# Joining even and odd halves before the last Fourier stage, moving adds from GpSimd to VectorE, and reordering loads and stores, in a kernel of gated attention and spectral mixing

## The chip, the cores and the metric

The kernel runs on one core of a Trainium2 chip. The metric is the device time of one execution in microseconds (us), lower is better. The core has five engines that run side by side, each through its own stream of instructions in order: TensorE (PE, matmuls), VectorE (DVE), ScalarE (ACT), GpSimd (POOL) and SyncE (SP, which here only issues DMAs). A program on one core is called slow in single executions that lie over 1.5% above the fastest of the same kernel; those are left out of every ratio.

## The reference

`x` has 2048 rows (S) and 640 columns (D). Two branches are mixed by a gate for each row:

```python
g = sigmoid((x * gate_w).sum(-1))          # one gate per row
out = g * A(x) + (1 - g) * B(x)

def A(x):   # 32 heads of 20, four segments of 512 rows, a running linear memory
    q, k, v = heads(x @ wq), heads(x @ wk), heads(x @ wv)
    phi = lambda t: where(t > 0, t + 1, exp(t))
    for s in range(4):
        p = softmax(qs @ ks.T * scale + causal_mask)
        o = sb * (phi(qs) @ M) / (phi(qs) @ z + 1e-6) + (1 - sb) * (p @ vs)   # sb = sigmoid(beta)
        M += phi(ks).T @ vs;  z += phi(ks).sum()
    return o @ wo

def B(x):   # mixing by a two-dimensional Fourier transform
    return irfft2(rfft2(x) * (w_r + 1j * w_i))
```

The Fourier transforms are done as matmuls with cosine and sine tables. Along the rows, 2048 = 128 x 16, in two stages each way; along d, with 321 frequencies.

## The kernel before

The kernel is written by a small list scheduler in Python. Over a thousand operations are recorded with what they read and write, with the engines they may run on, and with a priority. A table `PLAN` has 1,353 numbers, each of which shifts the priority of one operation.

Work by engine: PE does all matmuls; ACT the softmax exponentials (80 of 128x2048, 150 us) and some copies out of PSUM (the memory that matmuls write, in banks); POOL the causal masks (128, 81 us) and the adds shown below; DVE the rest.

The even and odd parts over d: the result of the inverse transform over d at columns d and 640-d is E+O and E-O. The kernel before keeps both, E at `G[..., 0:322]` and O at `G[..., 322:644]`, and lets the last Fourier stage (`Fb`) join them by accumulation, with a second table that carries the opposite sign for the second half:

```python
# inverse over d: n2 = 0..15, typ 0 is E, typ 1 is O; each is copied from PSUM by ACT or DVE
self.Sc.op(copy_alts(G.ap(n2 * 644 + typ * 322, [1, KD]), psum.ap(0, [1, KD])), name="ev_Db")

# last Fourier stage of an output tile (segment s, four token phases 4a..4a+3), for each half hf of the 640 columns
for typ in range(2):
    for q in range(4):      # 32x320 matmuls, one column group of PE each
        matmul(psum[32*q:32*q+32], fb.ap((L if hf and typ else 0) + 32 * (4*a + q), [1, 32]),
               G.ap((4*a + q) * 644 + typ * 322 + 320 * hf, [1 - 2*hf, 320]), start = typ == 0)
# ... then o @ wo is accumulated into the same bank, and the bank is copied to ot
dma(dap(out, (s*L + 4*a) * D, [D, 4], [16*D, 32], [1, D]), ot.ap(0, [1, D]), name="st_out")
```

phi(t) is max(t, 0) + min(exp(t), 1), in two DVE passes and one POOL add; the spectral product is two DVE products for each bank and POOL adds; the memory part of o is added on POOL:

```python
fmin: dve  et  = min(et, 1)
fmax: dve  dst = max(q, 0)
fadd: pool dst = dst + et
for r in range(2):
    W_mul: dve  Pt[2*r + ri] = psum * Wt[r]          # 128x321
W_add: pool Yt[r] = Pt[a0] -/+ Pt[a1]                # 128x321
addmem: pool on = on + mem                           # 128x320 (the last of 24 may run on DVE)
```

At the start, one transposed load brings the first segment of x; the weights follow, then eight loads of plain x for the Fourier branch (its first step are sums and differences of rows of x, "folds", on DVE and POOL). At the end, SP waits for every DMA semaphore.

The softmax here doesn't subtract the row's maximum and nothing guards it: scores larger than these inputs give would overflow.

## Time and profile before

| | before |
|---|---|
| time, median of fast runs | 273.74 us (272.74 to 275.2, 4 runs) |
| profiled span | 270.9 us |
| PE busy / DVE / ACT / POOL | 244.7 / 204.1 / 203.3 / 192.4 us |
| mean granted PE clock | 0.985 |
| end of the last copy to end of the span | 7.9 us (270.9 - 262.96) |

First lines of the profile's page: busy time by engine with its share of the span, and the span in 40 slices of 6.8 us, where each digit is tenths of busy (9 is 90% or more; for PEclk tenths of the full clock; for DMA the mean share of 16 DMA engines).

```profile
PE 244.7 (90%) x3354; PEld 145.4 (54%) x3376; DVE 204.1 (75%) x522; ACT 203.3 (75%) x207; POOL 192.4 (71%) x256
PE   8998698679999999998989999999999999999970
DVE  0179999979999989998999999889986653444300
POOL 7058887779697675899997968798999645535200
PEclk9999979999999999999999999999999999999996
DMA  7975975264985655875544456121651443374211
```

PE is the busiest engine, and its row shows where it is not busy: in the first fifth and in the last two slices.

The same by stretches of time: the two times of the stretch, its length, busy time of each engine with the number of instructions, granted clock, DMA share, GB/s.

```profile
core 0: us, PE busy (x) PEld busy (x) DVE busy (x) ACT busy (x) POOL busy (x), PEclk, DMA share, GB/s
0.00:20.00 20.00, 17.83 (x134) 6.62 (x137) 6.43 (x12) 8.52 (x10) 9.32 (x14) 1.00 0.87 243
20.00:40.00 20.00, 16.49 (x145) 8.86 (x146) 19.27 (x37) 11.13 (x17) 16.28 (x17) 0.91 0.81 201
40.00:60.00 20.00, 14.83 (x181) 8.24 (x179) 19.51 (x45) 14.56 (x19) 14.38 (x18) 1.00 0.46 127
60.00:200.00 140.00, 133.57 (x1755) 81.56 (x1773) 131.10 (x357) 121.70 (x117) 119.88 (x167) 1.00 0.56 138
200.00:262.50 62.50, 61.94 (x1148) 40.07 (x1145) 27.75 (x74) 46.96 (x47) 32.53 (x44) 1.00 0.39 88
```

From 20 to 60 us PE idles 8.7 of 40 us while DVE is busy 38.8. From 200 us on PE is busy nearly without a gap, so work taken from PE there should shorten the run. From 60 to 200 us PE is busy 95%, DVE 94%, and POOL 86%.

Groups of instructions (line, engine, operation, tiles, shapes, count, then busy us and mean ns, then idle time before them and its releaser), the POOL adds and one DVE pass:

```profile
L1030 POOL TENSOR_TENSOR phq<-phq,et_93 128x512 bf16<-128x512 bf16 x9 | 10.6, 1172 | 2.5 <-DVE et_93 L1028 2.5
L1307 POOL TENSOR_TENSOR Yt_68<-Pt_66 128x321 bf16<-128x321 bf16 x16 | 11.7, 739 | 3.2 <-DVE Pt_66 L1302 2.2 <-DVE rs_126 L1179 0.8
L1192 POOL TENSOR_TENSOR on_106<-on_106,mem 128x320 bf16<-128x320 bf16 x15 | 11.8, 795 | 0.8 <-DVE on_106 L1184 0.8
L1028 DVE TENSOR_SCALAR et_92<-et_92 128x512 bf16<-128x512 bf16 x15 | 8.5, 567 | 0.0
```

The timeline (start, length, engine, line, operation, tiles, count, then in brackets the idle time before it and its releaser): the first load of plain x, and the last two lines of the program.

```profile
9.78 0.53 SPq L596 DMA_DIRECT2D xsb<-in_A_x_dram  x1
...
262.52 0.44 ACT L575 ACTIVATE ot_77<-psum 128x320 bf16<-128x320 f32 x1 [0.24 <-PE psum L567]
262.99 0.54 SPq L596 DMA_DIRECT2D out_dram<-ot_77  x1
```

After the last issue, 7.4 us pass until the end. In the stretch from 262.5 to 266 us the DMA share is 0.26, at 84 GB/s.

### The profile page before, as it was taken

The page shows a single profiled execution, that of the slowest core. Times are in us where ns is not written, and L with a number is a line of the kernel's source. Part 1 is how long each engine was busy: PE and PEld are TensorE (multiplying, and loading weights), DVE is VectorE, ACT ScalarE, POOL GpSimd, SP SyncE. Part 2 cuts the span into 40 slices and gives each one's busy share as a digit, 9 for nine tenths or more (in the row PEclk, how much of TensorE's full clock was granted, in tenths as well). Part 3 has the DMA queues.
Part 4 walks back from the last instruction along what each step waited for, and adds up shares of the span by engine and source line. Part 5 has one row for each costly group of instructions (what it writes and reads, how often), then busy time and mean ns, then how long its engine had stood idle before and what let it go on. Part 6 is the DMA issues. An engine that isn't in the chain of part 4 may idle for free.

```text
span 270.9 us, 8271 instructions
## 1 busy us (share of the span) xinstructions
PE 244.7 (90%) x3354; PEld 145.4 (54%) x3376; DVE 204.1 (75%) x522; ACT 203.3 (75%) x207; POOL 192.4 (71%) x256
## 2 busy tenths in 40 slices
PE   8998698679999999998989999999999999999970
PEld 2333274445646565655546566646556646655770
DVE  0179999979999989998999999889986653444300
ACT  1467345988879889899789888979887888789440
POOL 7058887779697675899997968798999645535200
PEclk9999979999999999999999999999999999999996
DMA  7975975264985655875544456121651443374211
GB/s 193 311 231 168 232 178 160 68 161 91 232 189 131 147 141 164 200 133 150 135 115 126 121 165 201 52 70 43 175 147 58 129 71 78 84 118 96 63 50 60
DMA packets 55735, 36.83 MB, mean 136 GB/s; under 512 B 31521, under 2 KB 51985, under 8 KB 55697
## 3 DMA queue, kind: packets, MB, share of 16 engines
q1 hardware_dynamic: 54384, 35.81, 53.0%
q10 hardware_dynamic: 1312, 0.49, 0.7%
q8 instruction: 26, 0.43, 0.7%
q14 instruction: 13, 0.10, 0.1%
HBM read 19.90 MB, written 9.84 MB: 110 GB/s over the span
## 4 chain that ended last, share of the span: by engine, by line
PE 59%; DVE 24%; ACT 5%; POOL 4%; DMA 4%; issue 2%; DVEq 0%; SPq 0%
PE psum L567 59%; DVE xsb L877 4%; ACT ex L1149 3%; DMA gbc<-g_scr 2%; DVE phq L1029 2%; DVE qu_90 L577 2%; DVE et_93 L1028 1%; DVE et_92 L1028 1%; DMA k_scr<-qu_90 1%; DVE phk_95 L1029 1%; DVE xf_110 L872 1%; POOL fbg_72 L980 1%; DVE va_102 L1055 1%; POOL fbg_73 L980 1%; DVE Pt_67 L1302 1%
## 5 line engine op out<-in xcount | busy, mean ns | idle before, releaser
L1149 ACT ACTIVATE ex<-psum 128x2048 bf16<-128x2048 f32 x80 | 150.1, 1877 | 23.1 <-PE psum L567 22.4
L1152 POOL TENSOR_SCALAR_AFFINE_SELECT ex<-ex 128x512 bf16<-128x512 bf16 x128 | 81.0, 650 | 41.4 <-ACT ex L1149 37.8
L567 PEld LDWEIGHTS psum<-va_102,ex 128*128 128x128 bf16 x640 | 18.1, 96 | 4.1 <-POOL ex L1152 1.2
L567 PEld LDWEIGHTS psum<-va_103,ex 128*128 128x128 bf16 x640 | 18.3, 96 | 3.5 <-issue 0.8
L567 PE MATMUL psum<-va_103,ex 128*128 128x21 bf16 x640 | 19.1, 172 | 0.7 <-DVE Cp L577 0.5
L567 PE MATMUL psum<-va_102,ex 128*128 128x21 bf16 x640 | 19.2, 173 | 0.6 <-POOL ex L1152 0.5
L567 PE MATMUL psum<-big,Ac 128*128 128x161 bf16 (+2 forms) x96 | 17.8, 318 | 0.7 <-DVE Pt_67 L1302 0.5
L567 PE MATMUL psum<-qp_98,kp_100 20*128 20x512 bf16 (+3 forms) x256 | 15.8, 301 | 1.9 <-ACT ex L1149 1.2
L567 PE MATMUL psum<-wv,xT_88 128*128 128x500 bf16 (+1 forms) x80 | 14.8, 328 | 2.8 <-DVE va_102 L1055 2.7
L567 PE MATMUL psum<-big,Cp 128*128 128x321 bf16 (+1 forms) x96 | 16.2, 302 | 0.0
L567 PE MATMUL psum<-qp_99,kp_101 20*128 20x512 bf16 (+3 forms) x256 | 15.9, 301 | 0.2
L567 PE MATMUL psum<-xT_88,wk 128*128 128x512 bf16 (+1 forms) x85 | 14.7, 381 | 1.5 <-DVE q_70 L577 0.9
L1302 DVE TENSOR_TENSOR Pt_67<-psum,Wt_63 128x321 bf16<-128x321 f32 x32 | 14.6, 482 | 1.3 <-PE psum L567 1.1
L567 PE MATMUL psum<-wv,xT_89 128*128 128x500 bf16 (+1 forms) x80 | 14.3, 301 | 0.6 <-DVE Ac L577 0.6
L1302 DVE TENSOR_TENSOR Pt_66<-psum,Wt_62 128x321 bf16<-128x321 f32 x32 | 14.1, 481 | 0.7 <-PE psum L567 0.6
L577 DVE CAST G<-psum 128x321 bf16<-128x321 f32 x24 | 11.2, 490 | 4.4 <-PE psum L567 4.3
L567 PE MATMUL psum<-xT_88,wq 128*128 128x512 bf16 (+1 forms) x85 | 14.0, 380 | 0.4 <-issue 0.3
L1307 POOL TENSOR_TENSOR Yt_68<-Pt_66 128x321 bf16<-128x321 bf16 x16 | 11.7, 739 | 3.2 <-DVE Pt_66 L1302 2.2
L567 PE MATMUL psum<-xT_89,wq 128*128 128x512 bf16 x44 | 11.7, 381 | 0.9 <-DVE mem L1092 0.6
L1307 POOL TENSOR_TENSOR Yt_69<-Pt_67 128x321 bf16<-128x321 bf16 x16 | 11.5, 733 | 1.3 <-DVE Pt_67 L1302 1.3
L1192 POOL TENSOR_TENSOR on_106<-on_106,mem 128x320 bf16<-128x320 bf16 x15 | 11.8, 795 | 0.8 <-DVE on_106 L1184 0.8
L1030 POOL TENSOR_TENSOR phq<-phq,et_93 128x512 bf16<-128x512 bf16 x9 | 10.6, 1172 | 2.5 <-DVE et_93 L1028 2.5
(191 smaller groups left out, 548.2 us busy)
## 6 DMA issues: line engine op xcount, KB each, us to landing
xsb<-in_A_x_dram SPq DMA_DIRECT2D x8, 320.0 KB, 4.6
tt_59<-tab_tt SPq DMA_DIRECT2D x6, 256.0 KB, 3.8
q_scr<-qu_90 SPq DMA_DIRECT2D x6, 256.0 KB, 2.6
qp_99<-q_scr SPq DMA_DIRECT2D x16, 80.0 KB
kp_101<-k_scr SPq DMA_DIRECT2D x16, 80.0 KB
tt_60<-tab_tt SPq DMA_DIRECT2D x5, 256.0 KB
tt_61<-tab_tt SPq DMA_DIRECT2D x5, 256.0 KB, 3.1
o_scr<-on_105 SPq DMA_DIRECT2D x8, 160.0 KB
```

What stands on the lines that cost most here:

```text
L567: h = e.matmul(o_, l_, r_, start=st, stop=sp_, **kw)
L577: alts["dve"] = (lambda e: e.tensor_copy(dst(), src()), 75 + 1.04 * n, 85.0)
L877: self.either(lambda e, dst=dst, src=src, d0=d0, n=n, op=op: e.tensor_tensor(xs.ap(o + dst, [D, 2], [1, n]), xf.ap(src + d0, [321, 2], [1, ...
L980: fn = lambda e: e.tensor_tensor(fb.ap(0, [L, 2], [32, 16], [1, 32]), self.fcat.ap(256 + 32 * s, [P, 2], [0, 16], [1, 32]), self.gbc.ap(0, ...
L1028: fmin = lambda e: e.tensor_scalar(et.ap(0, [1, L]), et.ap(0, [1, L]), 1.0, None, ALU.min)
L1029: fmax = lambda e: e.tensor_scalar(dst(), qsl(), 0.0, None, ALU.max)
L1030: fadd = lambda e: e.tensor_tensor(dst(), dst(), et.ap(0, [1, L]), ALU.add)
L1149: self.one("act", lambda e: e.activation(dst(), src(), ACT.Exp, scale=SC), 4 * width, [bank], [self.exb(s, g, j) for g, j in outs], prio - ...
L1152: self.one("pool", lambda e, g=g, j=j: e.affine_select(self.ex.ap(self.exo(s, g) + JOFF[j], [1280, 4], [1, P]), self.ex.ap(self.exo(s, g) ...
L1192: add(*args, lambda e, g=g: e.tensor_tensor(on.ap(80 * g, [D, 4], [1, 80]), on.ap(80 * g, [D, 4], [1, 80]), self.mem.ap(80 * g, [D, 4], [1 ...
L1302: self.one("dve", lambda e, r=r, ri=ri, Pt=Pt, Wt=Wt, bank=bank: e.tensor_tensor(Pt.ap((2 * r + ri) * 322, [1, KD]), self.ps(bank, 0, [1, ...
L1307: fn = lambda e, r=r, a0=a0, a1=a1, op=op, Pt=Pt, Yt=Yt: e.tensor_tensor(Yt.ap(r * 322, [1, KD]), Pt.ap(a0 * 322, [1, KD]), Pt.ap(a1 * 322 ...
```

## The change

The intent: (1) join E and O by DVE while they leave PSUM, so that the last Fourier stage needs half of its matmuls; (2) take adds from POOL and give them to DVE, and pay for them on DVE with fewer, larger or fused passes; (3) bring plain x early, so that DVE has folds to do at once; (4) split the last stores by token phase over two queues, and wait at the end only for them; (5) a scheduler that knows a shared port of DVE and POOL, and a new `PLAN`, which now also picks the engine. The core of the diff, shortened:

```diff
 # (1) the inverse over d
-    copy_alts(G.ap(n2 * 644 + typ * 322, [1, KD]), psum)              # typ 0 and 1, ACT or DVE
+    if typ == 0:
+        copy_alts(eo.ap(0, [1, KD]), psum); continue                  # fp32, ACT or DVE
+    for q in range(2):                                                # DVE, into the joined G
+        tensor_tensor(G.ap(n2 * D + 639 * q, [1 - 2 * q, 320]), eo.ap(q, [1, 320]), psum.ap(q, [1, 320]),
+                      ALU.subtract if q else ALU.add)
 # (1) the last stage
-    for typ in range(2):
-        for q in range(4):
-            ... fb.ap((L if hf and typ else 0) + 32 * (4*a + q)), G.ap((4*a + q) * 644 + typ * 322 + 320 * hf, [1 - 2*hf, 320])
+    for q in range(4):
+        ... fb.ap(32 * (4*a + q), [1, 32]), G.ap((4*a + q) * D + 320 * hf, [1, 320])
 # (2) phi
-    fmax: dve tensor_scalar(dst, q, 0.0, None, max);  fmin: dve tensor_scalar(et, et, 1.0, None, min);  fadd: pool dst += et
+    fmax: dve tensor_scalar(dst, q, 0.0, 1.0, max, add);  fmin: dve tensor_tensor(dst, dst, et, min)
 # (2) spectral products and adds, memory adds
-    for r in range(2): dve Pt[2*r + ri] = psum * Wt[r]                # 128x321
+    dve Pt[ri, 2 + ri] = psum * Wt[0:2]                               # 128x642, psum read twice by a stride of 0
-    W_add: pool;  addmem: pool
+    W_add: dve or pool (23 and 9 by the plan);  addmem: dve or pool (20 and 4)
 # (3) loads
-    xt_load(0, 0.0)                       # all five chunks, ahead of wq and wk
+    xt_load(0, 0.0, 0, 3); xt_load(0, 0.01, 3, 2)      # behind the first parts of wq and wk; the plan puts plain x next
 # (4) last stores (s == 3)
-    dma(dap(out, (s*L + 4*a) * D, [D, 4], [16*D, 32], [1, D]), ot.ap(0, [1, D]))
+    for q in range(4):
+        dma(dap(out, (s*L + 4*a + q) * D, [16*D, 32], [1, D]), ot.ap(0, [1, D], p0=32*q, np_=32),
+            queue=("sp", "act", "sp", "act")[q])
-    for each DMA semaphore in use: sync.wait_ge(sem, count)
+    for each semaphore of the last stores: sync.wait_ge(sem, count)
 # (5) scheduler: lock of DVE and POOL, up to 1.6 MB of DMA in flight (1.0 before), new constants and PLAN   ... cut ...
```

By engine, DVE goes from 522 to 556 instructions and POOL from 256 to 175; PE loses 128 matmuls of 32x320.

## The prediction

> **What bounds it now.** TensorE: the page gives PE 244.7 us of a 270.9 us span (90%), DVE 204, ACT 203, POOL 192. By stretches PE is busy 95% from 60 to 200 us and practically 100% from 200 to 262.5 us (43.6 and 12.7 us unbroken in the chain of waits). Missing before the last copy: 1.3 us at the start, 10 us between 10 and 60 us, 6.5 us from 60 to 200. From 20 to 60 us DVE is the limit (busy 9.9, 9.3, 19.5 of 10, 10, 20 us); from 30 to 40 us the clock fell to 0.83. After the last matmul 8.4 us pass: the last stores move at 80 to 99 GB/s, DMA share 0.27.
>
> **What changes.**
> 1. Last Fourier stage: 256 matmuls of 32x320 become 128. Runs of 8 to 40 show one per 41 ns, so 5.3 us of PE go, all where PE has no idle time. DVE pays 32 sums of 128x320 from PSUM (like the 482 ns products), and 16 fp32 copies replace 32 copies of 490/440 ns: about +5 us DVE, from 193 to 222 us, where DVE has room (13.8 of 20 us).
> 2. POOL falls from 256 to 175 instructions. 30 phi adds (1.17 us each) go to DVE, 23 of 32 spectral adds (0.74), 19 of 23 memory adds (0.80), most of its folds: about 75 us off POOL. DVE gains some 30 us (0.32 us measured for one memory add), but loses 30 clamp passes (15 us) and 6 us from joining 64 products into 32. Today one shape of DVE tensor-scalar pass takes 0.22 to 1.48 us. The Trainium skill ("SBUF — State Buffer", "Who interferes with whom") says some DVE forms and GpSimd lock one port pair; the spread agrees. I expect DVE near 205 us still, POOL near 115.
> 3. Start: six early copies leave DVE for ACT, the first x load is split, folds come first on DVE, more bytes may be in flight. 15 warm-up matmuls stay ahead, so the first real one stays near 7 us. I give the PE gaps and clock loss before 60 us a gain of 4 us, those after 2 us. The weakest term.
> 4. End: each last store has outermost dimension 4. The Trainium skill ("DMA: Bandwidth & Descriptors", "Why a DMA increments its semaphore by 16 and not by 1") says a DMA takes the largest number of engines up to 16 that divides it: 4 of 16, which agrees with 0.27. Split by phase it is 32: 16 engines; two queues; only last stores are waited for. Tail 8.4 to about 4.5 us: -3.5 us.
>
> **Sum.** -5.3 -6 -3.5 = -15 us: 274.7 to 260 us, range 254.5 to 267. Steps 1 and 4 lie almost wholly on the critical path; of step 2 only what shows as fewer PE gaps counts. Chances: faster by over 2% 0.93, within 2% 0.06, slower 0.01.
>
> **What would show it.** PE busy near 239 us; 128 G matmuls at about 40 ns; no PE waits on G sums over 1 us; POOL near 115 us; tensor-scalar passes mostly under 0.5 us; last stores at a DMA share well over 0.27, last copy to end under 5 us; PE idle before the last copy 11 to 13 us instead of 18; clock 1.0 from 30 to 40 us.
>
> **What would make it wrong.** Folds first in DVE's order hold back V's evacuations and starve PE at 20 to 30 us; x loads ahead of wq delay projection; DVE, more loaded from 60 to 200 us, holds PSUM banks; the even copy, then sums, in series delay the last stage; stores on ACT's queue delay its copies.

## More of the kernel before

The scheduler then fixes the order on every engine at build time and puts semaphores in. So a change in one place can shift the order of everything, and the numbers in `PLAN` are fitted to one version of the kernel.

The count of matmuls (3354) is 22 short of that of weight loads (3376), so a few records are missing and PE's busy time is good to a few us only.

## The result, and the profile after

| | before | after |
|---|---|---|
| time, median | 273.74 us | 256.62 us (256.01 to 260.53, 4 runs) |
| ratio of fast runs, 95% interval | 1 | 0.9363 (0.9294 to 0.9432) |
| profiled span | 270.9 us | 255.2 us |
| PE / DVE / ACT / POOL busy | 244.7 / 204.1 / 203.3 / 192.4 | 241.7 / 203.2 / 202.8 / 114.2 us |
| mean granted PE clock | 0.985 | 0.993 |
| PE idle before the last copy | 17.8 us | 9.6 us |

A ratio is the mean time of one kernel's fast runs over the mean time of the other's fast runs of the same rounds, so it is not quite the ratio of the medians quoted. The change made the kernel faster by 17.1 us of the median, 6.4% by the ratio.

The page after, the same rows:

```profile
PE 241.7 (95%) x3248; PEld 142.3 (56%) x3248; DVE 203.2 (80%) x556; ACT 202.8 (79%) x208; POOL 114.2 (45%) x175
PE   7999989997999999989989999999998999999994
DVE  0799897768888999899999988989999984625543
POOL 8015634433532346745255748434665432416400
PEclk9999997999999999999999999999999999999999
DMA  7996979499449356746247484213565303553223
```

POOL's busy time fell by 78 us, that of DVE stayed the same. By stretches:

```profile
0.00:20.00 20.00, 18.68 (x134) 7.50 (x135) 11.73 (x37) 9.73 (x15) 5.79 (x10) 1.00 0.97 304
20.00:40.00 20.00, 19.20 (x208) 10.81 (x207) 18.34 (x46) 15.38 (x22) 10.68 (x13) 1.00 0.81 185
40.00:60.00 20.00, 17.94 (x244) 10.62 (x241) 13.99 (x38) 16.20 (x17) 7.98 (x13) 0.91 0.86 194
60.00:200.00 140.00, 134.57 (x1827) 81.39 (x1825) 129.87 (x366) 125.60 (x123) 72.17 (x112) 1.00 0.53 135
200.00:251.40 51.40, 51.35 (x853) 32.02 (x849) 29.29 (x73) 35.47 (x33) 17.56 (x27) 1.00 0.33 74
```

This table and that of before split up the 15.7 us by which the profiled span fell. Idle time of PE is the length of a stretch less its busy time:

| part of the span | before, us | after, us | difference | after, second profile |
|---|---|---|---|---|
| PE idle, 0 to 60 us | 10.85 | 4.18 | -6.7 | 4.02 |
| PE idle, 60 to 200 us | 6.43 | 5.43 | -1.0 | 7.59 |
| PE idle, 200 us to the last matmul | 0.56 | 0.05 | -0.5 | 0.00 |
| PE busy, whole span | 244.66 | 241.74 | -2.9 | 238.58 |
| after the last matmul | 8.4 | 3.8 | -4.6 | 3.8 |
| sum | 270.9 | 255.2 | -15.7 | 254.0 |

The last column is the same program in the run "The changed kernel again" below. It matters because the profile of before lacks 22 matmul records, 18 of them between 60 and 200 us, and so does the second profile of after, while the first lacks none. A missing record turns busy time into idle time. Like against like, PE's busy time fell by 6.1 us and its idle time from 60 to 200 us did not fall (6.43 to 7.59). So the -2.9 and the -1.0 are not findings; the -6.7 and the -4.6 stand in both profiles.

The largest term that stands in both is the idle time of PE in the first 60 us, where DVE now works 11.73 us in the first 20 us instead of 6.43. The mean clock rose for a reason that is worth nothing: each of the traces of before and after holds one stretch of 3.41 us at half clock while PE works (from 34.2 us before, from 41.0 us after); the other 4.6 us at half clock before lie after the last matmul, where they cost nothing.

The groups that took over the POOL adds:

```profile
L1063 DVE TENSOR_TENSOR phq<-phq,et 128x512 bf16<-128x512 bf16 x15 | 6.9, 473 | 0.5 <-ACT et L1051 0.5
L1334 DVE TENSOR_TENSOR Yt<-Pt 128x321 bf16<-128x321 bf16 x23 | 7.7, 351 | 0.0
L1220 DVE TENSOR_TENSOR on<-on,mem 128x320 bf16<-128x320 bf16 x20 | 8.4, 428 | 0.2
L1062 DVE TENSOR_SCALAR phq<-qu 128x512 bf16<-128x512 bf16 x15 | 5.5, 380 | 0.0
```

An add takes DVE half of what it took POOL (351 against 739 ns for a spectral add). The clamp passes over `et` are gone, and the 32 joined products take 25.6 us where the 64 single ones took 28.7 (14.6 and 14.1 us in two groups).

Timeline of the first loads of plain x, and of the end:

```profile
4.21 1.53 SPq L619 DMA_DIRECT2D xsb<-in_A_x_dram  x3
...
251.87 0.44 ACT L598 ACTIVATE ot<-psum 128x320 bf16<-128x320 f32 x1 [3.23 <-PE psum L590]
252.34 0.84 ACTq L619 DMA_DIRECT2D out_dram<-ot  x2
```

Plain x is asked for at 4.21 us instead of 9.78. After the last copy (end at 252.31 us) the program needs 2.9 us more instead of 7.9. The last copy itself is 0.5 us late: the last matmul ends at 251.35, and ACT was still issuing stores.

### The profile page after: what moved, and what is told of

It is laid out like the page before. It is cut to its first block, busy times and chain, and to the rows that moved or that the text cites. A ratio compares the mean times of both kernels' runs of the same rounds, so it can differ in the third digit from the quotient of the medians.

```text
span 255.2 us, 7980 instructions
## 1 busy us (share of the span) xinstructions
PE 241.7 (95%) x3248; PEld 142.3 (56%) x3248; DVE 203.2 (80%) x556; ACT 202.8 (79%) x208; POOL 114.2 (45%) x175
## 4 chain that ended last, share of the span: by engine, by line
PE 78%; DVE 7%; DMA 5%; ACT 3%; SPq 2%; issue 1%; POOL 1%; ACTq 0%; DVEq 0%
PE psum L590 78%; DMA pkn<-phk 3%; ACT ex L1180 2%; SPq L619 2%; DVE Pt L1329 2%; DMA tt<-tab_tt 1%; DMA kp<-k_scr 1%; DVE va L1086 1%; DVE mem L1123 1%; POOL Yt L1334 1%; DVE Cp L600 1%; DVE G L1375 1%; ACT eo L598 1%; DVE qu L600 1%; POOL ex L1183 1%
## 5 line engine op out<-in xcount | busy, mean ns | idle before, releaser
L590 PEld LDWEIGHTS psum<-va,ex 128*128 128x128 bf16 x1280 | 36.7, 96 | 6.7 <-issue 1.5
L590 PE MATMUL psum<-va,ex 128*128 128x21 bf16 x1280 | 38.6, 172 | 1.0 <-POOL ex L1183 0.3
L590 PE MATMUL psum<-qp,kp 20*128 20x512 bf16 (+3 forms) x512 | 31.9, 303 | 1.4 <-DMA kp<-k_scr 0.8
L590 PE MATMUL psum<-xT,wk 128*128 128x512 bf16 (+1 forms) x140 | 28.6, 381 | 1.3 <-DVE qu L600 0.8
L590 PE MATMUL psum<-xT,wq 128*128 128x512 bf16 (+1 forms) x140 | 28.3, 381 | 0.2 <-DVE Pt L1329 0.2
L590 PE MATMUL psum<-wv,xT 128*128 128x141 bf16 (+1 forms) x160 | 28.0, 306 | 0.0
L1329 DVE TENSOR_TENSOR Pt<-psum,Wt 128x642 bf16<-128x642 f32 x32 | 25.6, 821 | 2.1 <-PE psum L590 1.9
L590 PE MATMUL psum<-wo,oT 128*128 128x320 bf16 x120 | 22.1, 301 | 0.0
L1051 ACT ACTIVATE et<-qu 128x512 bf16<-128x512 bf16 x25 | 15.6, 630 | 2.7 <-DVE qu L600 2.5
L1375 DVE TENSOR_TENSOR G<-eo,psum 128x320 bf16<-128x320 f32 x32 | 14.6, 475 | 2.5 <-PE psum L590 2.4
L590 PEld LDWEIGHTS psum<-xT,wq 128*128 128x128 bf16 (+1 forms) x140 | 10.3, 98 | 11.2 <-issue 1.6
L1215 DVE TENSOR_TENSOR on<-psum,rs 128x320 bf16<-128x320 f32 x32 | 15.4, 482 | 0.3
L590 PE MATMUL psum<-tt,Yt 128*128 128x256 bf16 (+1 forms) x96 | 15.3, 276 | 0.1
```

What stands on the lines that cost most here:

```text
L590: h = e.matmul(o_, l_, r_, start=st, stop=sp_, **kw)
L1051: self.one("act", lambda e: e.activation(et.ap(0, [1, L]), qsl(), ACT.Exp), L, [qb], [b("et", pi_)], late, name="phi_exp")
L1215: self.one("dve", lambda e, rs=rs, bank=bank, g=g: e.tensor_tensor(on.ap(80 * g, [D, 4], [DH, 4], [1, DH]), self.ps(bank, 0, [88, 4], [VW, ...
L1329: self.one("dve", lambda e, ri=ri, Pt=Pt, Wt=Wt, bank=bank: e.tensor_tensor(Pt.ap(ri * 322, [644, 2], [1, KD]), self.ps(bank, 0, [0, 2], [ ...
L1375: self.one("dve", lambda e, q=q, n2=n2, bank=bank, eo=eo: e.tensor_tensor(self.G.ap(n2 * D + 639 * q, [1 - 2 * q, 320]), eo.ap(q, [1, 320] ...
```

## The experiments

All runs below had five rounds unless said otherwise, beside runs of the kernel before on the same chip. To compare two changed kernels, the difference of their ratios to the kernel before is multiplied by 273 us. This is needed where two kernels ran on different chips. "Order kept" means that the order of instructions on each engine was that of the kernel changed, apart from the edit. Where the scheduler ran anew, it is said. All outputs agreed with the reference within its tolerance.

The theory after the result: the gain is four separate things, namely less PE work, a shorter tail, an earlier start of the folds, and POOL freed while DVE's total load stays as it was. The rival for each: it did not matter, because the new plan or another part gave the gain. A rival to the last: POOL was not in the way before, only DVE's load counts.

### The changed kernel again

> Control: the changed kernel once more, so that the other runs of this call have a partner on the same chip. Expected 256 to 257 us, ratio to before 0.936.

Measured: 256.07 us, ratio 0.9374 (0.9336 to 0.9411), span 254.0 us, PE busy 238.6, DVE 203.1, POOL 115.0. This is the base for what follows. PE's busy time differs by 3 us between two profiles of the same program. In this one 22 of 3248 matmul records are missing. So PE's busy time cannot carry a statement about a few us unless as many records are missing on both sides.

### The last stage twice

```diff
-            for q in range(4):
+            for q in (0, 1, 2, 3) * 2:      # the second set starts the same sums anew: same result, 128 matmuls more
```

> The changed kernel with each of the 32 sets of 4 last-stage matmuls issued twice (the second set overwrites the first, result unchanged), order of all else kept. Theory (that stretch is bound by TensorE, each extra matmul costs its 41 ns): +4.5 to +5.3 us over the changed kernel. Rival (TensorE's busy time fell only from 244.7 to 241.7 us, so the halving saved 3 us at most, the rest came from elsewhere): +3 us or less. Second rival (the stretch is bound by the exponentials, the halving hidden): under +1 us.

Measured: 260.4 us, 0.9527 (0.9488 to 0.9566), so 0.0153 x 273 = +4.2 us for 128 matmuls, or 33 ns each. By the two intervals this is good to about 1.5 us, so it lies between what the theory (4.5 to 5.3) and the first rival (3 or less) had said, and rules out only the second (under 1). (The order of PE's weight loads is that of the kernel changed but for the second sets.) So the halving is worth about 4 us, nearly all of it on the critical path.

Why 33 ns and not the 41 of the prediction can be read from the traces. A set of the last stage and the matmul that follows it, first before, then after:

```profile
236.58 0.46 PE L567 MATMUL psum<-G,fbg_74 128*32 128x320 bf16 x8
236.97 0.31 PE L567 MATMUL psum<-wo,oT_81 128*128 128x320 bf16 x1
221.88 0.32 PE L590 MATMUL psum<-G,fbg 128*32 128x320 bf16 x4
222.13 0.85 PE L590 MATMUL psum<-wo,oT 128*128 128x320 bf16 x5
```

From its start to the next matmul a set of eight takes 0.39 us, a set of four 0.25 (the medians of the sets that stand alone, too). Four matmuls less save 0.14 us, or 35 ns each; about 0.11 us comes once for each unbroken run (a run of 16 took 0.66 us). All sets together take 10.95 us before and 6.95 after: 4.0 us less. The 41 ns were the whole time of a run divided by its matmuls, and with sets of four that becomes 54 ns.

### The last stores whole again

```diff
-        for q in range(4):
-            dma(dap(out, (s*L + 4*a + q) * D, [16*D, 32], [1, D]), ot.ap(0, [1, D], p0=32*q, np_=32), queue=("sp", "act", "sp", "act")[q])
+        dma(dap(out, (s*L + 4*a) * D, [D, 4], [16*D, 32], [1, D]), ot.ap(0, [1, D]))
```

> The changed kernel with the four last stores whole again (one DMA of 4x32x640 each, on SP), still waiting for the last stores only. Theory (4 of 16 DMA engines, near 97 GB/s): +2 to +4 us, DMA share in the last 4 us back near 0.25, last copy to end 5 us or more in place of 2.9. Rival (the tail's gain came from waiting for fewer semaphores): under +1 us.

Measured: 259.97 us, 0.9527 (0.9482 to 0.9573), so +4.2 us, at the upper end of what the theory had said; the rival (under 1 us) fails. (The scheduler ran anew and three late copies changed between ACT and DVE. The short wait list was kept.) The stretches after its last matmul:

```profile
250.00:252.00 2.00, 0.00 (x0) 0.00 (x0) 0.00 (x0) 0.27 (x1) 0.00 (x0) 1.00 0.27 89
252.00:254.00 2.00, 0.00 (x0) 0.00 (x0) 0.00 (x0) 0.00 (x0) 0.00 (x0) 0.53 0.26 84
```

and the same stretch of the changed kernel in its second profile:

```profile
250.00:252.00 2.00, 0.20 (x8) 0.00 (x0) 0.00 (x0) 0.44 (x1) 0.00 (x0) 1.00 0.47 129
```

A whole store moves at a DMA share of 0.26 to 0.27, about 4 of 16 engines, and the split ones at 0.47. The Trainium skill ("DMA: Bandwidth & Descriptors", "Why a DMA increments its semaphore by 16 and not by 1") says that a DMA uses the largest number up to 16 that divides the slowest dimension of both access patterns. Here that is 4 for the whole store and 16 for a split one. The 0.27 agrees with the 4; the 0.47 lies well above it, but does not show 16. The last copy ends at 250.27 us here, and the span at 257.3: 7.0 us of tail against 2.9. The edit undoes the split and the second queue at once; which of the two brings the gain was not taken apart.

### The moved adds back on POOL

```diff
+ for o in schedule.order:                       # after scheduling: same order, other engine
+     if o.name in ("W_add", "addmem", "phi_min"): o.eng = "pool"
- fmin: dve tensor_tensor(dst, dst, et, min)
+ fmin: pool tensor_tensor(dst, dst, et, add)    # an add in place of the minimum: phi is wrong on purpose; the output still passed the comparison
```

> The changed kernel with 73 adds (30 of phi, 23 spectral, 20 of memory) moved from DVE to POOL after the scheduling, the order of everything kept (phi's minimum becomes an add, which POOL can run, so the result is wrong on purpose). POOL should read about 185 to 190 us busy, DVE 175 to 180. Theory (both engines are off the critical path; only latency and the port wait come back): +1 to +4 us. Rival (the relief of POOL is what made the kernel faster): +6 us or more. If DVE was the hidden limit: faster.

Measured: 264.04 us, 0.9637 (0.9593 to 0.9681), so 0.0263 x 273 = +7.2 us. This is what the rival had said (+6 or more), not the theory (+1 to +4). Busy: DVE 189.1 (14 less), POOL 176.5 (61 more). Waits of PE on POOL (wait in us in total, count, longest), first of this kernel:

```profile
PE psum L590 <- POOL ex L1187: 3.8, 3, 2.7
PE psum L590 <- POOL Yt L1338: 1.2, 2, 0.9
```

then of the kernel changed:

```profile
PE psum L590 <- POOL ex L1183: 0.3, 1, 0.3
```

`ex` written by POOL are the causal masks. POOL is busy only 68% of the time, and DVE even lost work, but an add of 0.7 to 1.2 us that stands in POOL's queue ahead of a mask makes PE wait for the mask. In the longest wait, of 2.7 us, a memory add of 0.83 us and a phi add of 1.15 us run just ahead of the masks and among them. These waits account for 5.0 us, less 0.3 that were there before (0.6 in its second profile), of the 7.2. The rest is not placed; one more cost is that passes which stayed on DVE became longer, phi's first pass over q from 380 to 512 ns. So loading POOL costs time long before its share of busy time says so.

This is the cost of load on POOL in the new order, not what its relief gained over the kernel before. There PE's waits for masks were 1.5 us in four waits, and no other wait for POOL is listed, while its listed waits for DVE were 12.2 us; in the kernel changed these are 0.3 and 7.0 (listed are causes of 0.2 us or more in total). So the rival, that POOL was not in the way before and only DVE's load counts, is not excluded; POOL can have cost time there through DVE, whose passes over one shape took 0.22 to 1.48 us.

### POOL busy beside DVE, with reads and without

Two kernels leave the adds on DVE, and give POOL dummy operations beside them, one add or two memsets for each of the 73, of about the same POOL time (63.3 and 58.6 us more than in the kernel changed). One has adds that read and write a scratch tile; the other has memsets that only write it. Order kept.

```diff
+ for each DVE op in (W_add, addmem, phi_min):
+     d_tt:  pool tensor_tensor(scratch, scratch, scratch, add)      # 321, 340 or 512 columns
+     d_mem: pool memset(scratch), twice                             # 512+120, 512+180 or 512+480 columns
```

> The changed kernel with a dummy add on POOL (scratch tile only, 0.74 to 1.17 us each) placed beside each of 73 adds that stay on DVE; order kept, result right. POOL should read 175 to 190 us busy. Theory (the 7 us that moving the adds to POOL cost came from POOL being occupied: masks wait in its queue, and DVE waits for the shared port): +5 to +8 us, DVE busy above 203 us. Rival (they came from the longer time of the adds themselves on the way from product to next matmul): +0 to +2 us.

> The same dummies as memsets (write only, read nothing), of about the same time on POOL. If the queue in front of the masks is what costs, the same as the dummy adds within 1 us. If it is the port that POOL's reading shares with DVE's second input, less than half of their loss, and DVE's adds near 0.3 to 0.4 us.

Measured: with adds, 277.11 us, 1.0131 (1.0073 to 1.0189), +20.7 us over the kernel changed, far more than the theory (+5 to +8) or its rival had said. With memsets, 262.88 us, 0.9638 (0.9571 to 0.9706), +7.2 us, less than half of that, as was expected if the port is what costs. The profile of the first fell in a single execution of 732.7 us, in which matmuls of 512 columns took 1.05 to 1.10 us instead of 0.38; its trace holds no record of the clock, so the 1.0 listed for it is no measurement. It says nothing of the others, so this kernel was looked at again with one round:

> A second look at the kernel with dummy adds on POOL, since its profile fell in an execution of 732 us in which every matmul was slow. Expected 275 to 278 us again, DVE over 215 us busy (its two-input adds wait for POOL's reads), clock 0.96 to 0.975, with TensorE idle 20 us or more. If DVE stays at 203 to 208 us, the port is not the reason.

Measured: 277.11 us (two runs), 1.0147 (1.0089 to 1.0204); DVE busy 227.3, POOL 178.3, clock 0.969. Its DVE adds, whose own work is unchanged:

```profile
L1355 DVE TENSOR_TENSOR Yt<-Pt 128x321 bf16<-128x321 bf16 x23 | 13.8, 614 | 0.0
L1241 DVE TENSOR_TENSOR on<-on,mem 128x320 bf16<-128x320 bf16 x20 | 13.0, 659 | 0.2
```

and those of the kernel with memsets, with one single-input pass:

```profile
L1355 DVE TENSOR_TENSOR Yt<-Pt 128x321 bf16<-128x321 bf16 x23 | 8.2, 372 | 0.0
L1241 DVE TENSOR_TENSOR on<-on,mem 128x320 bf16<-128x320 bf16 x20 | 9.0, 456 | 0.2
L1083 DVE TENSOR_SCALAR phq<-qu 128x512 bf16<-128x512 bf16 x15 | 8.5, 580 | 0.0
```

The Trainium skill ("SBUF — State Buffer", "Who interferes with whom") says: "A DVE instruction with two SBUF inputs contends with a GpSimd instruction that reads SBUF, not with one that only writes it". The runs agree: 351 ns becomes 614 with readers and 372 with writers. It also says that passes in a two-port form contend with GpSimd, and makes no exception there for writers; the single-input pass of 380 ns that became 580 beside memsets agrees, if it runs in that form, which the trace does not show.

Two things follow. First, 24 us more of DVE time (227.3 - 203.1) make the run 21 us longer. The trace shows the way: PE's listed waits for DVE rise from 7.2 us (second profile of the kernel changed) to 21.5, those for masks stay at 0.5, and PE's own busy time is 7 us longer at the lower clock. So DVE has little slack for more work; that less work on DVE would make this kernel faster is not shown by it. Second, memsets that share no data with anything cost 7.2 us. That includes 5.5 us more DVE time (208.6) and the waits of PE for masks, which rise to 3.8 us again. How the 7.2 us divide between these two, this run does not tell. In the run with the adds back on POOL, DVE's load as a whole fell, so there the queue of POOL is the likelier cause.

### Loads in the old order

```diff
- xt_load(0, 0.0, 0, 3); xt_load(0, 0.01, 3, 2)
+ xt_load(0, 0.0)                                 # in one piece
- ld_x: priority 1.0
+ ld_x: priority 3.3                              # plain x behind the weights
```

> The changed kernel, scheduled anew, with the start's loads undone: first transposed x load in one piece, the eight plain x loads after the weights instead of ahead of them. Theory (the folds start earlier because x comes first, which empties DVE's queue before 60 us, where the changed kernel has 4 us of TensorE idle instead of 11): +3 to +6 us, TensorE idle before 60 us 7 us or more. Rival (the order of TensorE's work made the start's gain, not the loads): under +2 us.

Measured: 267.45 us, 0.9785 (0.9736 to 0.9833), so 0.0411 x 273 = +11.2 us. All theories had expected less. The scheduler ran anew here, and PE's weight loads differ in their tiles at 688 of 3248 places. Plain x is asked for at 6.97 us. The stretches:

```profile
0.00:20.00 20.00, 18.09 (x118) 7.46 (x119) 5.61 (x19) 7.29 (x13) 5.13 (x9) 1.00 0.99 270
20.00:40.00 20.00, 14.14 (x106) 6.70 (x104) 19.41 (x55) 11.50 (x20) 10.49 (x9) 1.00 1.05 245
40.00:60.00 20.00, 17.38 (x241) 10.07 (x242) 13.49 (x33) 17.14 (x20) 6.28 (x10) 1.00 0.74 168
```

The picture of the kernel before is back: DVE does 5.61 us of work in the first 20 us (11.73 with the early loads) and is full in the next 20, and PE idles 10.4 us in the first 60 us (1.91 + 5.86 + 2.62), against 4.2 with the early loads and 10.85 in the kernel before. So 6.2 us of the 11.2 are this idle time. The other 5 us come later, and how much of them is a plan that no longer fits, rather than the loads, stays open.

### The three structural parts without the new plan

To the kernel before were added the joined E and O, the fused phi with joined products and free choice for the adds, and the split stores with the short wait list. Loads, scheduler rules and `PLAN` stayed old. The scheduler ran anew.

```diff
  before.py
+ (1) joined E and O, one pass of the last stage
+ (2) fused phi, products of 2 x 321, adds on DVE or POOL
+ (4) split last stores, short wait list
```

> The kernel before, with its old loads, plan and order rules, plus the three structural parts: joined halves with single last stage, adds and phi's minimum on DVE with joined products, split last stores with short final wait. If these parts make the whole gain: 256 to 259 us. If the loads at the start and the new plan have a share of their own: 261 to 267 us.

Measured: 288.37 us, 1.044 (1.0327 to 1.0553), slower than before by 0.044 x 273 = 12 us. Four of its six runs are slow against its own fastest of 283.58, so the interval rests on two. This missed what all had expected. DVE is busy 215.6 us and POOL 134.9, with engines chosen by the old rules, which do not know the shared port; the clock is 0.948; and its last copies waited 4 to 5.5 us for a store of their own buffer. From here to the kernel changed it is (1.044 - 0.9374) x 273 = 29 us, which the loads, the scheduler's rules and the new plan bring together. So the parts are worth what they are worth only with an order made for them. Which of the three hurt most was not taken apart.

### Adds from POOL to DVE, in the kernel before

```diff
+ for o in schedule.order:                       # of the kernel before, order kept
+     if o.name in ("W_add", "addmem", "phi_add"): o.eng = "dve"
```

> The kernel before, order kept, with its 85 adds on POOL (30 phi, 32 spectral, 23 of memory) moved to DVE: the reverse of the move in the other direction. POOL about 110 us, DVE 215 to 225. If relief of POOL is worth 7 us by itself: -4 to -8 us against before. If DVE is the limit of the kernel before (20 to 60 us) and the relief pays only together with the shorter phi and the new order: -2 to +6 us.

Measured: 278.55 us, 1.0196 (1.0165 to 1.0226), so +5.3 us, within the -2 to +6 that were expected if DVE is the limit. POOL falls from 192 to 122 us, DVE rises from 204 to 217.9. So freeing POOL alone, in the old order and with DVE paying for it, loses. In the kernel changed the same move costs DVE nothing in total, because fused phi and joined products give the time back. That it is this pair that helps is argued from here; no run undoes the fusing alone.

### Two attempts to go further

```diff
  # both: the last two copies on DVE (ACT is busy issuing stores); the last four warm-up matmuls cut to 64 columns
- final copies: act;  warm-up k = 12..15: 512 columns
+ final copies: dve;  warm-up k = 12..15: 64 columns
  # the second one too: the remaining 13 POOL adds on DVE
+ W_add, addmem: dve
```

> The changed kernel, order kept, with the very last copy on DVE instead of ACT (where it waits behind two store issues for about 0.5 us) and the last four warm-up matmuls cut from 512 to 64 columns. If the first x load and weights have landed by 6.2 us, TensorE's real work starts 1.2 to 1.5 us earlier: together -1 to -2 us against the changed kernel. If they land at 7.4 us: only the 0.5 us of the end. If the shorter warm-up leaves the clock low: slower by 1 us or more.

> As imp1, and the 13 adds that the plan left on POOL (9 spectral, 4 of memory) go to DVE as well, order kept. If POOL's time is what the masks wait for, another -0.5 to -1.5 us; if DVE (93% busy from 60 to 200 us) has become the limit there: 0 to +2 us against imp1.

Measured: the first 255.88 us, 0.937 (0.933 to 0.941), which is not told apart from the kernel changed (0.9374); the 1 to 2 us that were hoped for did not come. With the shorter warm-up the first real matmul started at 6.67 us instead of 6.95 (second profile of the kernel changed), after a wait for x:

```profile
6.67 2.34 PE L591 MATMUL psum<-xT,wk 128*32 128x512 bf16 x40 [0.91 <-DMA xT<-in_A_x_dram]
```

The second: 256.8 us, 0.9416 (0.9382 to 0.945), 1.3 us above the first by the ratios, with intervals that still overlap. DVE's busy time is 206.2, 3 us more than in the kernel changed, which fits that added DVE time shows but does not prove it, and 13 adds on POOL are a reasonable place to stop. No version was found that clearly beats the kernel changed.

## Why the prediction was right

The total was right: 260.0 us was said with a range of 254.5 to 267, and 256.62 was measured, 2.4 us better in gain (17.1 against 14.7 us from the stated 274.7). By term:

| term of the sum | predicted | measured |
|---|---|---|
| 1. halved last stage | -5.3 us | -4.2 us, by doing it twice; -4.0 us in the traces |
| 2 and 3. PE gaps and clock before 60 us | -4 us | -6.7 us in the profile's idle time, nothing in the clock; loads in the old order bring 6.2 back |
| 2 and 3. PE gaps after 60 us | -2 us | not shown: -1.5 us by one profile, +0.6 by the other |
| 4. tail | -3.5 us | -4.2 us by undoing it, -4.6 us in the profile |

The mechanisms of terms 1 and 4 held, with sizes near. That the total came so near is in part luck: term 1 and the gaps after 60 us were put too high, the start and the tail too low, and this cancels. And the sum has no term for the scheduler and the plan, without which, and without the early loads, the other parts made the kernel 12 us slower. What did the work can be read from the traces: 6.7 us of idle time at the start, 4.6 of tail and 4.0 of last-stage matmuls are 15.3 of the 15.7 us.

The most mis-sized term is the one that the prediction called "the weakest term", the start. It gave "the PE gaps and clock loss before 60 us a gain of 4 us", with a true reason (folds first on DVE, the x load split), and the idle time fell by 6.7. What it had not drawn from the profile is how much work DVE could do before 20 us if it had data: the row of before shows 6.43 us busy of 20, and then 38.8 of 40. Work brought forward into that hole no longer stands ahead of PE's banks at 20 to 60 us; the run with the old loads supports this, though its order changed too.

One sentence was too weak. "From 20 to 60 us DVE is the limit" is right, but it leaves the impression that DVE has room after. Its load of 93 to 94% from 60 to 200 us leaves little, as 24 us more on DVE made the run 21 us longer. And the prediction counted of POOL's relief "only what shows as fewer PE gaps", without saying how it would show. Moving 73 adds back costs 7.2 us, about half of it through masks that stand behind adds in POOL's queue.

The signs that were named: POOL near 115 (114.2), DVE near 205 (203.2), PE busy near 239 (241.7 in one profile, 238.6 in another), no wait on the sums of E and O over 1 us (the longest 0.5), tensor-scalar passes mostly under 0.5 us (380 ns here, about 290 for those of k), DMA share at the end well over 0.27 (0.47 in the second profile), last copy to end under 5 us (2.9) all came. The matmuls of the last stage were to take about 40 ns each and took 54, counted with the fixed part of a set. PE's idle time before the last copy was to be 11 to 13 us and was 9.6. The clock was to be 1.0 from 30 to 40 us; it was, but it read 0.63 from 40 to 44 us instead, so that loss moved rather than went away.

Two of the risks that were named did not come: folds first did not starve PE (19.20 of 20 us busy from 20 to 40), and DVE's load from 60 to 200 us did not grow (131.10 to 129.87). One came in part: ACT's stores delay its last copy, by 0.5 us.

The costs of undoing the four parts, 4.2 + 4.2 + 7.2 + 11.2 = 26.8 us, exceed the gain of 17.1. They are not additive, as each undone part leaves the rest with an order fitted to the whole. What stays open: what the new plan and the scheduler's rules bring by themselves, the share of the plan in the 11.2 us of the loads, the shares of the second queue and of the short wait list in the tail, and the execution of 732.7 us.

## What to carry to other kernels

When work moves between VectorE and GpSimd, look at two things and not at shares of busy time: whether VectorE's total stays the same (fuse or join something to pay for what comes), and which short operation, on which TensorE waits, stands behind the moved work in GpSimd's queue. An engine that idles at the start and is full right after can be a sign that its data come late: order the loads by whose backlog they open. Test single moves with the order of instructions kept; a structure and the plan made for it can only be judged together.

## What the Trainium skill lacked or had wrong

- "SBUF — State Buffer", "Who interferes with whom", has the rule for two SBUF inputs right, but gives no size for such an add. Here, beside GpSimd adds, a 128x321 add on VectorE went from 351 to 614 ns, a 128x320 one from 428 to 659; beside memsets they took 372 and 456.
- "Perfetto Trace Analysis", "Optimizing Scalar/DVE Operations", says that offloading from a saturated VectorE to GpSimd may make sense, but that between these two it "might not help", because of the shared port. Here it cost 7.2 us although VectorE's busy time fell by 14 us; the largest waits that grew were those behind GpSimd's queue (masks, 0.3 to 3.8 us), which the section does not mention. Its own reason shows too: a pass that stayed on VectorE went from 380 to 512 ns.
- "TensorE: Matmul & The Clock Gate", Part 1, says that the clock falls after an idle window of about 3.4 us, and tells further down of a kernel whose clock oscillated with short idles of PE. In the kernel changed it fell to 0.5 for 3.41 us, at 41.04 us in one profile and at 53.77 in the other, though PE was not idle longer than 0.78 and 0.57 us at a time between 20 us and there. So the first rule does not give these falls; whether the short idles do, no run here settles.
